# Decode attention over a long K/V cache: last chunk moved into the common loops, fewer score signals, VectorE loop head at slot 128, mask set by GpSimd

## The chip, the cores and the metric

The kernel runs on one core of a Trainium2 chip. The metric is device time in microseconds (us), median of several executions. Besides the time, each kernel left a profile of one execution: busy times, waits, and the start and end of every instruction and of every DMA packet. Engines are PE (TensorE matmuls), PEld (TensorE weight loads), DVE (VectorE), ACT (ScalarE), POOL (GpSimd) and SP (SyncE, which here only issues transfers). "SPq" and "DVEq" are the sequencers of those engines.

## The reference

One token, 16 query heads, 8 K/V heads, a cache of 65,536 positions by 256 values, all bf16. Attention is mixed by a scalar gate with a small MLP, which GpSimd and ScalarE do on the side and which plays no part in the argument.

```python
q = (x @ wq).reshape(B, Sq, Hq, Dh)                    # 16 heads of 256, D = 448
scores = einsum("bhqd,bhkd->bhqk", q, k) * Dh ** -0.5  # k, v: 8 heads, each for 2 query heads
p = softmax(scores)
a = einsum("bhqk,bhkd->bhqd", p, v).reshape(...) @ wo
out = g * a + (1 - g) * mlp(x)                         # g = sigmoid((x * gate_w).sum())
```

K and V together are 537 MB, read once. Next to that the arithmetic is small.

## The kernel before

The cache is cut into 48 chunks: 8 heads ("turns") of 6 chunks each, with 6, 6, 5, 5, 5 and 5 steps of 2048 positions. There are two K buffers and one V buffer. For each chunk VectorE transposes K step by step into three small buffers `kT`, TensorE computes 8 score matmuls per step, ScalarE takes the exponential, VectorE transposes the result, and TensorE multiplies it by V. VectorE's addition of that product (`drain_pv`) raises `s_vf`; this releases the V buffer, and SyncE then issues the next V and K loads together.

```python
def load_k(i):
    if i >= 2: sp.wait_ge(s_vf, i - 1)
    sp.dma_start(out=kbuf[i % 2][...], in_=kv_src(A_k_cache, i))
def load_v(i):
    if i >= 1: sp.wait_ge(s_vf, i + 1)
    sp.dma_start(out=vbuf[...], in_=kv_src(A_v_cache, i))

plan = [(0, 1), (1, 2), (2, 0), (3, 1), (5, 2), (4, 0)]   # (step, kT buffer)
def turns(i):                                             # VectorE
    take(dve, s_k[i % 2], 16)                             # K chunk landed
    for t, (s, b) in enumerate(blocks(i)):
        if t >= 3:                                        # a kT buffer is used again
            take(dve, s_s, 6 - steps[i] + 1 if t == steps[i] - 1 else 1)
        dve.transpose(out=kT[b], in_=step s of K).then_inc(s_kt, 1)
# scores(): steps 0, 1 and 2 each raise s_s when their last matmul is done

with nc.Fori(0, HKV, 1, engines=[DVE], head_slot={DVE: 0}) as turn_v:
    for c in range(PER):
        turns(c)
        ...                                               # drain_pv -> s_vf; transpose of p -> s_pt
# TensorE: loop over 47 chunks (scores 0..3, p_v of the chunk before, last scores);
# the 48th chunk is written out again after the loop, with its own probability buffer
```

`head_slot` is the loop's parameter for the slot at which its first instruction is placed. The rest of the kernel is unchanged, apart from its tail shown in the diff.

The softmax here doesn't subtract the row's maximum and nothing guards it: scores larger than these inputs give would overflow.

Of the kernel before, what the change touches and what calls it, by code (L numbers as in the profile page):

```python
# [9 lines left out]
BF16 = mybir.dt.bfloat16  # L10
# [5 lines left out]
HKV = 8  # L16
DH = 256
# [77 lines left out]
def kernel(  # L95
# [78 lines left out]
    pT_t = [const.tile([128, 512], BF16, name=f"pT{i}") for i in range(2)]  # L174
# [32 lines left out]
    def critical():  # L207
# [12 lines left out]
        s_d = nc.alloc_semaphore("s_d")  # L220
        s_g = nc.alloc_semaphore("s_g")
# [52 lines left out]
        )  # L274
        do("pool", lambda e: e.memset(block[:], 0.0), writes=["block"])
# [5 lines left out]
        do("pool", lambda e: e.memset(ymix[:], 0.0), writes=["ymix"])  # L281
        for t, key, val in (
            (one_b, "one_b", 1.0), (xd, "xd", 0.0), (one_f, "one_f", 1.0), (zero_b, "zero_b", 0.0),
            (xw, "xw", 0.0), (pat, "pat", 0.0), (qw, "qw", 0.0), (col_f, "col_f", 1.0), (pv, "pv", 0.0),
        ):
            do("dve", lambda e: e.memset(t[:], val), writes=[key])
# [141 lines left out]
        for m, spans in offsets.items():  # L428
            for lo, hi in spans:
                do("dve", lambda e: e.memset(pat[:, m, lo:hi], 1.0), writes=["pat"])  # L430
# [91 lines left out]
        def turns(i):  # L522
            kn = kbuf[i % 2][:].bitcast(FP32)
            take(dve, s_k[i % 2], 16)
            for t, (s, b) in enumerate(blocks(i)):
                if t >= 3:
                    take(dve, s_s, 6 - steps[i] + 1 if t == steps[i] - 1 else 1)
                dve.transpose(  # L528
                    out=kT[b][:].bitcast(FP32), in_=kn[:, s * SB * 128:(s + 1) * SB * 128]
                ).then_inc(s_kt, 1)  # L530
# [32 lines left out]
        with nc.Fori(0, HKV, 1, engines=[DVE], head_slot={DVE: 0}) as turn_v:  # L563
            for c in range(PER):
                turns(c)
                if c == 0:
                    with dve.If_ne(t_reg, 0):
                        take(dve, s_pv)
                        take(dve, s_d)
                        drain_pv(False).then_inc(s_vf, 1)  # L570
                        dve.memset(tick[:], 0.0).then_inc(s_g, 1)
                    with dve.Else():
                        dve.memset(og[:], 0.0).then_inc(s_vf, 1)
                    take(dve, s_e)
                    dve.transpose(out=pT_t[0][:], in_=p_t[:]).then_inc(s_pt, 1)  # L575
                    with dve.If_ne(t_reg, 0):
                        take(dve, s_o)
                        rden_gate(o_ps[:, 0, 2:4])
                        take(dve, s_wo, 16)
                        heads().then_inc(s_ot, 1)  # L580
                elif c < PER - 1:
                    take(dve, s_pv)
                    drain_pv(c == 1).then_inc(s_vf, 1)
                    take(dve, s_e)
                    dve.transpose(out=pT_t[0][:], in_=p_t[:]).then_inc(s_pt, 1)  # L585
                else:
                    with dve.If_lt(t_reg, HKV - 1):
                        take(dve, s_pv)
                        drain_pv(False).then_inc(s_vf, 1)
                        take(dve, s_e)  # L590
                        dve.transpose(out=pT_t[0][:], in_=p_t[:]).then_inc(s_pt, 1)  # L591
                        for r in range(2):
                            queries(turn_v + 1, r)
                        den_rows()
                        dve.tensor_scalar(
                            out=og[:], in0=og[:], scalar1=dsum[:, 0:1], scalar2=None, op0=ALU.add
                        ).then_inc(s_d, 1)
                    with dve.Else():
                        take(dve, s_e)
                        dve.transpose(out=pT_t[1][:], in_=p_t[:]).then_inc(s_pt, 1)  # L600
            dve.reg_add(t_reg, t_reg, 1)
# [54 lines left out]
        def scores(s, b, first, last):  # L656
            pe.wait_ge(s_kt, 1).then_inc(s_kt, -1)  # L657
            kv = kT[b][:].rearrange("p (j b y two) -> p j b y two", j=SB, b=4, two=2)
            at = PAD - ROW0 - s
            for q in range(8):  # L660
                ins = pe.matmul(  # L661
                    sc[:], lhsT=qw[:, q, at:at + 128], rhs=kv[:, :, q // 2, :, q % 2],
                    start=(first and q == 0), stop=(last and q == 7), skip_group_check=True,
                )
            if last:
                ins.then_inc(s_sc, 1)
            elif s < 3:
                ins.then_inc(s_s, 1)
# [29 lines left out]
        g_reg = pe.alloc_register("g_reg")  # L698
        f_reg = pe.alloc_register("f_reg")
        pe.reg_mov(c_reg, 0)  # L700
        pe.reg_mov(v_reg, PER)
        pe.reg_mov(g_reg, PER + 1)
        pe.reg_mov(f_reg, 1)
        with nc.Fori(0, total - 1, 1, engines=[PE], head_slot={PE: 0}):
            for s, b in plan[0:4]:
                scores(s, b, s == 0, False)
            with pe.If_lt(f_reg, 1):
                pe.wait_ge(s_pt, 1).then_inc(s_pt, -1)
                pe.wait_ge(s_v, 16).then_inc(s_v, -16)  # L709
                for s in range(4):  # L710
                    p_v(vbuf, pT_t[0], s, s == 0, False)
                with pe.If_lt(v_reg, big):
                    p_v(vbuf, pT_t[0], 5, False, False)
                p_v(vbuf, pT_t[0], 4, False, True).then_inc(s_pv, 1)
            pe.reg_mov(f_reg, 0)
# [3 lines left out]
            pe.reg_mov(v_reg, c_reg)  # L719
            pe.reg_add(c_reg, c_reg, 1)  # L720
            with pe.If_eq(c_reg, PER):
                pe.reg_mov(c_reg, 0)
            pe.reg_add(g_reg, g_reg, -1)
            with pe.If_lt(g_reg, 1):
                pe.reg_mov(g_reg, PER)
                pe.wait_ge(s_g, 1).then_inc(s_g, -1)
                o_turn(4).then_inc(s_o, 1)
                pe.wait_ge(s_ot, 1).then_inc(s_ot, -1)  # L728
                for k in range(4):
                    cc, r = divmod(k, 2)  # L730
                    ins = pe.matmul(  # L731
                        acc[0:1, 0:D], lhsT=oT[:, k:k + 1], rhs=wo[:, r, cc, :], start=False,
                        stop=False, skip_group_check=True,
                    )
                ins.then_inc(s_oo, 1)

# [3 lines left out]
        for t, (s, b) in enumerate(blocks(last_i)):  # L740
            scores(s, b, t == 0, t == steps[-1] - 1)
        take(pe, s_pt)
        take(pe, s_v, 16)
        for s in range(steps[-2]):
            p_v(vbuf, pT_t[0], s, s == 0, False)
        then(dve.tensor_tensor(out=dmul[:], in0=den[:], in1=dmask, op=ALU.mult))
        dve.tensor_reduce(out=dsum[:], in_=dmul[:], axis=AXIS.X, op=ALU.add).then_inc(s_fd, 1)
        pe.wait_ge(s_fd, 1)
        pe.matmul(
            den_ps[:, 0:2], lhsT=dsum[:].to_broadcast([128, 128]), rhs=mask[:, D0:D0 + 2, 0],  # L750
            start=True, stop=True,
        ).then_inc(s_fp, 1)
        pe.wait_ge(s_mp, 6 * NF)
        pe.matmul(
            acc[0:1, 0:D], lhsT=col_f[:], rhs=ymix[:], start=False, stop=True, skip_group_check=True,
        ).then_inc(s_fp, 1)
        dve.wait_ge(s_fp, 1)
        rden_gate(den_ps[:, 0:2])
        dve.wait_ge(s_fp, 2)
        dve.tensor_scalar(  # L760
            out=row[:], in0=acc[0:1, 0:D], scalar1=bias[:, 0:1], scalar2=None, op0=ALU.add
        ).then_inc(s_fd, 1)

        pTk = pT_t[1][:].rearrange("p (i b x) -> p i b x", b=4, x=16)
        pTr = pT_t[1][:].rearrange("p (j r x) -> p j r x", r=2, x=16)

        def upright(lo, hi):
            for jj in range(lo, hi, 2):
# [4 lines left out]
                    rhs=vlast[:, jj * DH:(jj + 2) * DH], start=False, stop=jj >= nlast - TURN - 8,  # L773
# [14 lines left out]

        take(pe, s_pt)
        pe.wait_ge(s_last[0], 16)  # L790
        upright(edges[0], edges[1])
        pe.wait_ge(s_fd, 2)
# [5 lines left out]
        pe.wait_ge(s_last[1], 16)  # L798
        upright(edges[1], edges[2]).then_inc(s_fp, 1)
        dve.wait_ge(s_fp, 3)  # L800
        drain_pv(False).then_inc(s_fd, 1)
        pe.wait_ge(s_fd, 3)
        o_turn(2)
        pe.wait_ge(s_last[2], 16)
        turned(edges[2], edges[3])
        pe.wait_ge(s_last[3], 16)
        turned(edges[3], edges[4]).then_inc(s_fp, 1)
        dve.wait_ge(s_fp, 4)
        heads().then_inc(s_fd, 1)
        pe.wait_ge(s_fd, 4)  # L810
# [11 lines left out]
        dve.wait_ge(s_fp, 5)  # L822
        dve.tensor_copy(out=res[0:97, :], in_=acc4[0:97, 0:DQ]).then_inc(s_fd, 1)  # L823
        s_out = nc.alloc_semaphore("s_out")
        sp.wait_ge(s_fd, 5)
# [37 lines left out]
```

## Time and profile before

| what | number |
|---|---|
| time, median of the first 3 runs | 1268.05 us (1266.36 to 1268.35) |
| span of the profiled run | 1264.1 us |
| HBM read | 544.22 MB, 431 GB/s over the span |

These lines are from the page of the kernel before: busy time and share of the span, the DMA row in 40 slices (9 is 90% or more), and the K/V queue.

```profile
PE 721.0 (57%) x4296; PEld 282.0 (22%) x4296; DVE 666.8 (53%) x471; ACT 50.1 (4%) x127; POOL 76.7 (6%) x98
DMA  9999999999999999999999999999999999999998
q1 hardware_dynamic: 16744, 544.22, 99.7%
```

No compute engine is busy much over half of the time. The queue that carries K and V is busy throughout. The table by window (columns: window, length, busy time of each engine with instruction counts, granted TensorE clock, DMA share, GB/s) says the same for the stretches between the two ends, again for the kernel before:

```profile
20.00:100.00 80.00, 46.03 (x244) 17.37 (x243) 48.29 (x29) 2.71 (x7) 1.69 (x2) 0.80 1.01 434
100.00:1220.00 1120.00, 639.52 (x3768) 249.36 (x3767) 590.84 (x381) 44.48 (x113) 72.17 (x81) 0.78 1.00 434
```

One steady chunk of the kernel before, in the timeline (start, length, engine, line, operation, count, and in brackets the idle time before it with what ended it):

```profile
1211.07 8.89 DVE L528 STREAM_TRANSPOSE kT<-kbuf 128x2048 f32<-128x2048 f32 x4 [6.34 <-DVEq L520]
1213.53 9.39 PE L661 MATMUL sc<-kT,qw 128*128 128x512 bf16 x32 [10.38 <-PEq L657]
1221.34 2.31 DVE L528 STREAM_TRANSPOSE kT<-kbuf 128x2048 f32<-128x2048 f32 x1 [1.37 <-DVEq L520]
1225.65 0.69 DVE L539 TENSOR_TENSOR og<-pv,og 128x512 f32<-128x512 f32 x1 [2.00 <-DVEq L520]
1226.37 0.33 SPq L247 DMA_DIRECT2D vbuf<-in_A_v_cache_dram  x1
```

VectorE waits 6.34 us for K to land, does four transpositions without a break, and 14.6 us after the first one the drain releases the next V load. In the same timeline the start of the program and the end look like this; the second line is the third K chunk's load, the third the second V chunk's:

```profile
31.50 13.28 DVE L528 STREAM_TRANSPOSE kT<-kbuf 128x2048 f32<-128x2048 f32 x6 [5.82 <-DVEq L520]
45.35 0.34 SPq L241 DMA_DIRECT2D kbuf<-in_A_k_cache_dram  x1
63.13 0.33 SPq L247 DMA_DIRECT2D vbuf<-in_A_v_cache_dram  x1
...
1258.84 1.43 PE L782 MATMUL misc<-pT,kbuf 128*128 128x2 bf16 x48 [0.56 <-DMA kbuf<-in_A_v_cache_dram]
1260.30 0.16 DVE L546 TENSOR_TENSOR oT<-misc,rden 128x4 bf16<-128x4 f32 x1 [3.18 <-PE misc L782]
1260.52 0.54 PE L816 MATMUL acc<-wo,oT 128*1 128x112 bf16 x16 [0.25 <-DVE oT L546]
1261.11 0.28 DVE L823 CAST res<-acc 97x112 bf16<-97x112 f32 x1 [0.65 <-PE acc L816]
```

After the last V rows land at about 1258.8 us, 5.3 us remain to the end of the span.

A number used below is the **cover** of an issue. It is the time from the issue of a V chunk to the landing of the last packet of the K chunk queued ahead of it, read from the trace's packet records. While the cover is well above zero, the queue has bytes left when the new load arrives. In the kernel before, the second V chunk, issued at 63.1 us, has a cover of 6.8 us. From the ninth V chunk on the least is about 6.3 and the median about 8.4 us (there from the landing signals, which in these traces come 0.3 to 0.5 us after the last packet).

### The profile page before, as it was taken

What the parts mean: (1) busy time and instruction counts of PE and PEld (TensorE: products, weight loads), DVE (VectorE), ACT (ScalarE), POOL (GpSimd) and SP (SyncE); (2) the same over time, 40 slices, a digit from 0 to 9 for tenths busy, and PEclk for the clock granted to TensorE, in tenths of its full rate; (3) what the DMA queues carried; (4) which work ended last, traced back from release to release, by engine and by line L of the source; (5) the groups of instructions that cost most, each with busy time, mean ns of one, the idle gap of its engine ahead of it and who ended that gap; (6) DMA issues with size and microseconds to landing.
All of it is one profiled execution on the core that took longest, in us unless ns stands there. A gap on an engine that the chain in (4) does not pass through costs nothing. (4 is left out here: it accounts for less than half of the span.)

```text
span 1264.1 us, 10739 instructions
## 1 busy us (share of the span) xinstructions
PE 721.0 (57%) x4296; PEld 282.0 (22%) x4296; DVE 666.8 (53%) x471; ACT 50.1 (4%) x127; POOL 76.7 (6%) x98
## 2 busy tenths in 40 slices
PE   3755655456555665556554564566645755456556
PEld 1321222122221222212221221222212222122212
DVE  4845555365544645455555554465545654466444
ACT  0000000000000000000000000000000000000000
POOL 0001010110101101001011011000000000000000
PEclk9876788778777787777887788777877787778887
DMA  9999999999999999999999999999999999999998
GB/s 407 424 439 430 437 438 425 438 434 428 440 437 423 434 436 433 440 430 435 434 429 435 430 435 440 430 429 437 430 440 435 430 431 435 427 443 435 424 435 350
DMA packets 16842, 544.32 MB, mean 431 GB/s; under 512 B 1856, under 2 KB 3906, under 8 KB 4162
## 3 DMA queue, kind: packets, MB, share of 16 engines
q1 hardware_dynamic: 16744, 544.22, 99.7%
q8 instruction: 3, 0.05, 0.0%
q14 instruction: 5, 0.04, 0.0%
q10 hardware_dynamic: 90, 0.01, 0.0%
HBM read 544.22 MB, written 0.00 MB: 431 GB/s over the span
## 5 line engine op out<-in xcount | busy, mean ns | idle before, releaser
L661 PE MATMUL sc<-kT,qw 128*128 128x512 bf16 x2048 | 564.5, 438 | 458.6 <-PEq L657 458.6
L528 DVE STREAM_TRANSPOSE kT<-kbuf 128x2048 f32<-128x2048 f32 x256 | 571.1, 2283 | 310.7 <-DVEq L520 310.7
L661 PEld LDWEIGHTS sc<-kT,qw 128*128 128x128 bf16 x2048 | 213.7, 108 | 807.7 <-issue 644.1
L675 PE MATMUL pv<-vbuf,pT 128*4 128x512 bf16 x2008 | 130.5, 412 | 54.6 <-PEq L709 54.2
L539 DVE TENSOR_TENSOR og<-pv,og 128x512 f32<-128x512 f32 x39 | 27.0, 692 | 108.8 <-DVEq L520 106.3
L675 PEld LDWEIGHTS pv<-vbuf,pT 128*4 128x4 bf16 x2008 | 50.6, 92 | 132.4 <-issue 92.9
L608 ACT ACTIVATE p_t<-sc 128x512 bf16<-128x512 f32 x48 | 28.7, 597 | 1190.0 <-PE sc L661 1190.0
L585 DVE STREAM_TRANSPOSE pT<-p_t 128x512 bf16<-128x512 bf16 x32 | 22.8, 711 | 74.3 <-DVEq L520 74.3
L635 POOL TENSOR_SCALAR t_b<-t_b 128x448 f32<-128x448 f32 x14 | 7.9, 566 | 359.9 <-ACT t_b L617 359.9
L639 POOL TENSOR_SCALAR t_b<-t_b,hw 128x448 f32<-128x448 f32 x14 | 9.0, 640 | 333.4 <-ACT t_b L625 333.4
L538 DVE COPY og<-pv 128x512 f32<-128x512 f32 x8 | 5.5, 692 | 35.4 <-DVEq L520 35.4
L575 DVE STREAM_TRANSPOSE pT<-p_t 128x512 bf16<-128x512 bf16 x8 | 5.7, 711 | 26.9 <-DVEq L520 26.9
L644 POOL TENSOR_TENSOR ymix<-ymix,t_b 128x448 f32<-128x448 f32 x14 | 16.1, 1149 | 1.1
L643 POOL TENSOR_TENSOR t_b<-t_b,u_b 128x448 f32<-128x448 f32 x14 | 15.8, 1128 | 1.2
L638 POOL TENSOR_TENSOR t_b<-t_b,u_b 128x448 f32<-128x448 f32 x14 | 15.8, 1127 | 1.2
L731 PE MATMUL acc<-wo,oT 128*1 128x448 bf16 x28 | 7.0, 374 | 12.7 <-PEq L728 12.7
L591 DVE STREAM_TRANSPOSE pT<-p_t 128x512 bf16<-128x512 bf16 x7 | 5.0, 711 | 13.1 <-DVEq L520 13.1
L617 ACT ACTIVATE t_b<-h_bc,b1T,w1T 128x448 f32<-128x448 f32 x14 | 10.5, 747 | 0.0
L631 POOL TENSOR_SCALAR u_b<-h_bc,w1T,b1T 128x448 f32<-128x448 f32 x14 | 10.0, 718 | 4.1 <-DVE pat L430 2.7
L608 ACT ACTIVATION_READ_ACCUMULATOR p_t<-sc 128x1 f32 x48 | 9.3, 194 | 0.0
L685 PEld LDWEIGHTS misc<-mask,og 128*128 128x128 f32 x64 | 8.7, 196 | 2.3 <-DVE og L539 1.3
L448 PE MATMUL sc<-vbuf,xw 128*128 128x512 bf16 x32 | 9.0, 449 | 0.0
(89 smaller groups left out, 70.3 us busy)
## 6 DMA issues: line engine op xcount, KB each, us to landing
kbuf<-in_A_k_cache_dram SPq DMA_DIRECT2D x32, 5120.0 KB, 33.2
vbuf<-in_A_v_cache_dram SPq DMA_DIRECT2D x31, 5120.0 KB, 20.8
kbuf<-in_A_k_cache_dram SPq DMA_DIRECT2D x16, 6144.0 KB, 36.1
vbuf<-in_A_v_cache_dram SPq DMA_DIRECT2D x16, 6144.0 KB, 24.2
wo<-in_A_wo_dram SPq DMA_DIRECT2D x7, 448.0 KB, 22.3
vbuf<-in_A_wq_dram SPq DMA_DIRECT2D x1, 3072.0 KB, 10.2
kbuf<-in_A_v_cache_dram SPq DMA_DIRECT2D x1, 2560.0 KB, 26.5
kbuf<-in_A_v_cache_dram SPq DMA_DIRECT2D x1, 1280.0 KB, 31.1
```

The costliest lines, as they stand in the source:

```text
L448: last = e.matmul(q_ps[:], lhsT=xw[:, k, HKV - 1 - n:HKV - 1 - n + 128], rhs=rhs, start=(n == 0 and k == 0), stop=(n == HKV - 1 and k >= K ...
L528: dve.transpose(out=kT[b][:].bitcast(FP32), in_=kn[:, s * SB * 128:(s + 1) * SB * 128]).then_inc(s_kt, 1)
L539: return dve.tensor_tensor(out=og[:], in0=pv[:], in1=og[:], op=ALU.add)
L585: dve.transpose(out=pT_t[0][:], in_=p_t[:]).then_inc(s_pt, 1)
L608: ins = act.activation(out=p_t[:], in_=sc[:], func=ACT.Exp, scale=scale, accum_out=den[:, c:c + 1])
L617: ins = act.activation(out=t_b[:], in_=h_bc[:], func=ACT.Square, scale=w1T[:, b:b + 1], bias=b1T[:, b:b + 1],)
L631: lambda: pool.tensor_scalar(out=u_b[:], in0=h_bc[:], scalar1=w1T[:, b:b + 1], scalar2=b1T[:, b:b + 1], op0=ALU.mult, op1=ALU.add,),
L638: lambda: pool.tensor_tensor(out=t_b[:], in0=t_b[:], in1=u_b[:], op=ALU.mult),
L643: lambda: pool.tensor_tensor(out=t_b[:], in0=t_b[:], in1=u_b[:], op=ALU.mult),
L644: lambda: pool.tensor_tensor(out=ymix[:], in0=ymix[:], in1=t_b[:], op=ALU.add),
L661: ins = pe.matmul(sc[:], lhsT=qw[:, q, at:at + 128], rhs=kv[:, :, q // 2, :, q % 2], start=(first and q == 0), stop=(last and q == 7), ski ...
L675: ins = pe.matmul(pv[32 * a:32 * a + 4, :], lhsT=pT[:, k, :, ROW0 + s], rhs=vt[:, j * DH:(j + 2) * DH], start=first and k < 4, stop=last a ...
```

## The change

The intent is to run all 48 chunks through one TensorE loop and one VectorE loop body, with fewer signals and less VectorE work in the preamble. The diff, cut to its core:

```diff
-with nc.Fori(0, HKV, 1, engines=[DVE], head_slot={DVE: 0}) as turn_v:
+with nc.Fori(0, HKV, 1, engines=[DVE], head_slot={DVE: 128}) as turn_v:
 ...
-                if t >= 3:
-                    take(dve, s_s, 6 - steps[i] + 1 if t == steps[i] - 1 else 1)
+                if t in (3, steps[i] - 1):
+                    take(dve, s_s)
 ...  in scores():
-            elif s < 3:
+            elif s in (1, 2):
                 ins.then_inc(s_s, 1)
 ...  VectorE, sixth chunk of a turn: the special case of the last turn is gone;
 ...  denominator rows now come ahead of the next head's queries
 ...  TensorE
-        with nc.Fori(0, total - 1, 1, engines=[PE], head_slot={PE: 0}):
+        with nc.Fori(0, total, 1, engines=[PE], head_slot={PE: 0}):
-        for t, (s, b) in enumerate(blocks(last_i)):
-            scores(s, b, t == 0, t == steps[-1] - 1)
-        ...  p_v of chunk 46
 ...  tail: drain of chunk 46 is in the loop, so upright() starts a new sum (start=jj < 8);
 ...  the four matmuls on `row` move from between the two upright() calls to after turned()
 ...  preamble: the 11 memsets of `pat`, and those of zero_b and col_f, on GpSimd, not VectorE
```

With three signals, transposition 3 (the fourth) waited for score step 0. With two, it waits for score step 1, since one signal is now counted for both.

More of the change, by code (lines that the diff above doesn't have):

```diff
@@ L173 @@
     p_t = const.tile([128, 512], BF16, name="p_t")
-    pT_t = [const.tile([128, 512], BF16, name=f"pT{i}") for i in range(2)]
+    pT = const.tile([128, 512], BF16, name="pT")
     den = const.tile([128, PER], FP32, name="den")
@@ L220, in critical @@
         s_d = nc.alloc_semaphore("s_d")
+        s_dn = nc.alloc_semaphore("s_dn")
         s_g = nc.alloc_semaphore("s_g")
@@ L274, in critical @@
         )
+        do("pool", lambda e: e.memset(pat[:], 0.0), writes=["pat"])
+        for m, spans in offsets.items():
+            for lo, hi in spans:
+                do("pool", lambda e: e.memset(pat[:, m, lo:hi], 1.0), writes=["pat"])
         do("pool", lambda e: e.memset(block[:], 0.0), writes=["block"])
@@ L281, in critical @@
         do("pool", lambda e: e.memset(ymix[:], 0.0), writes=["ymix"])
+        do("pool", lambda e: e.memset(zero_b[:], 0.0), writes=["zero_b"])
+        do("pool", lambda e: e.memset(col_f[:], 1.0), writes=["col_f"])
         for t, key, val in (
-            (one_b, "one_b", 1.0), (xd, "xd", 0.0), (one_f, "one_f", 1.0), (zero_b, "zero_b", 0.0),
-            (xw, "xw", 0.0), (pat, "pat", 0.0), (qw, "qw", 0.0), (col_f, "col_f", 1.0), (pv, "pv", 0.0),
+            (one_b, "one_b", 1.0), (xd, "xd", 0.0), (xw, "xw", 0.0), (one_f, "one_f", 1.0),
+            (qw, "qw", 0.0), (pv, "pv", 0.0),
         ):
@@ L425, in critical @@
         )
-        for m, spans in offsets.items():
-            for lo, hi in spans:
-                do("dve", lambda e: e.memset(pat[:, m, lo:hi], 1.0), writes=["pat"])
         do(
@@ L568, in critical @@
                         take(dve, s_pv)
-                        take(dve, s_d)
+                        take(dve, s_dn)
                         drain_pv(False).then_inc(s_vf, 1)
@@ L574, in critical @@
                     take(dve, s_e)
-                    dve.transpose(out=pT_t[0][:], in_=p_t[:]).then_inc(s_pt, 1)
+                    dve.transpose(out=pT[:], in_=p_t[:]).then_inc(s_pt, 1)
                     with dve.If_ne(t_reg, 0):
@@ L584, in critical @@
                     take(dve, s_e)
-                    dve.transpose(out=pT_t[0][:], in_=p_t[:]).then_inc(s_pt, 1)
+                    dve.transpose(out=pT[:], in_=p_t[:]).then_inc(s_pt, 1)
                 else:
-                    with dve.If_lt(t_reg, HKV - 1):
-                        take(dve, s_pv)
-                        drain_pv(False).then_inc(s_vf, 1)
-                        take(dve, s_e)
-                        dve.transpose(out=pT_t[0][:], in_=p_t[:]).then_inc(s_pt, 1)
-                        for r in range(2):
-                            queries(turn_v + 1, r)
-                        den_rows()
-                        dve.tensor_scalar(
-                            out=og[:], in0=og[:], scalar1=dsum[:, 0:1], scalar2=None, op0=ALU.add
-                        ).then_inc(s_d, 1)
-                    with dve.Else():
-                        take(dve, s_e)
-                        dve.transpose(out=pT_t[1][:], in_=p_t[:]).then_inc(s_pt, 1)
+                    take(dve, s_pv)
+                    drain_pv(False).then_inc(s_vf, 1)
+                    take(dve, s_e)
+                    dve.transpose(out=pT[:], in_=p_t[:]).then_inc(s_pt, 1)
+                    den_rows()
+                    dve.tensor_scalar(
+                        out=og[:], in0=og[:], scalar1=dsum[:, 0:1], scalar2=None, op0=ALU.add
+                    ).then_inc(s_dn, 1)
+                    for r in range(2):
+                        queries(turn_v + 1, r)
             dve.reg_add(t_reg, t_reg, 1)
@@ L697, in critical @@
         v_reg = pe.alloc_register("v_reg")
-        g_reg = pe.alloc_register("g_reg")
-        f_reg = pe.alloc_register("f_reg")
         pe.reg_mov(c_reg, 0)
         pe.reg_mov(v_reg, PER)
-        pe.reg_mov(g_reg, PER + 1)
-        pe.reg_mov(f_reg, 1)
-        with nc.Fori(0, total - 1, 1, engines=[PE], head_slot={PE: 0}):
+        with nc.Fori(0, total, 1, engines=[PE], head_slot={PE: 0}):
             for s, b in plan[0:4]:
                 scores(s, b, s == 0, False)
-            with pe.If_lt(f_reg, 1):
+            with pe.If_lt(v_reg, PER):
                 pe.wait_ge(s_pt, 1).then_inc(s_pt, -1)
@@ L710, in critical @@
                 for s in range(4):
-                    p_v(vbuf, pT_t[0], s, s == 0, False)
+                    p_v(vbuf, pT, s, s == 0, False)
                 with pe.If_lt(v_reg, big):
-                    p_v(vbuf, pT_t[0], 5, False, False)
-                p_v(vbuf, pT_t[0], 4, False, True).then_inc(s_pv, 1)
-            pe.reg_mov(f_reg, 0)
+                    p_v(vbuf, pT, 5, False, False)
+                p_v(vbuf, pT, 4, False, True).then_inc(s_pv, 1)
             with pe.If_lt(c_reg, big):
@@ L718, in critical @@
             scores(4, 0, False, True)
-            pe.reg_mov(v_reg, c_reg)
-            pe.reg_add(c_reg, c_reg, 1)
-            with pe.If_eq(c_reg, PER):
-                pe.reg_mov(c_reg, 0)
-            pe.reg_add(g_reg, g_reg, -1)
-            with pe.If_lt(g_reg, 1):
-                pe.reg_mov(g_reg, PER)
+            with pe.If_eq(v_reg, PER - 1):
                 pe.wait_ge(s_g, 1).then_inc(s_g, -1)
@@ L735, in critical @@
                 ins.then_inc(s_oo, 1)
+            pe.reg_mov(v_reg, c_reg)
+            pe.reg_add(c_reg, c_reg, 1)
+            with pe.If_eq(c_reg, PER):
+                pe.reg_mov(c_reg, 0)
         s_fd = nc.alloc_semaphore("s_fd")
         s_fp = nc.alloc_semaphore("s_fp")
-        for t, (s, b) in enumerate(blocks(last_i)):
-            scores(s, b, t == 0, t == steps[-1] - 1)
-        take(pe, s_pt)
-        take(pe, s_v, 16)
-        for s in range(steps[-2]):
-            p_v(vbuf, pT_t[0], s, s == 0, False)
-        then(dve.tensor_tensor(out=dmul[:], in0=den[:], in1=dmask, op=ALU.mult))
-        dve.tensor_reduce(out=dsum[:], in_=dmul[:], axis=AXIS.X, op=ALU.add).then_inc(s_fd, 1)
-        pe.wait_ge(s_fd, 1)
-        pe.matmul(
-            den_ps[:, 0:2], lhsT=dsum[:].to_broadcast([128, 128]), rhs=mask[:, D0:D0 + 2, 0],
-            start=True, stop=True,
-        ).then_inc(s_fp, 1)
-        pe.wait_ge(s_mp, 6 * NF)
-        pe.matmul(
-            acc[0:1, 0:D], lhsT=col_f[:], rhs=ymix[:], start=False, stop=True, skip_group_check=True,
-        ).then_inc(s_fp, 1)
-        dve.wait_ge(s_fp, 1)
-        rden_gate(den_ps[:, 0:2])
-        dve.wait_ge(s_fp, 2)
-        dve.tensor_scalar(
-            out=row[:], in0=acc[0:1, 0:D], scalar1=bias[:, 0:1], scalar2=None, op0=ALU.add
-        ).then_inc(s_fd, 1)
-        pTk = pT_t[1][:].rearrange("p (i b x) -> p i b x", b=4, x=16)
-        pTr = pT_t[1][:].rearrange("p (j r x) -> p j r x", r=2, x=16)
+        pTk = pT[:].rearrange("p (i b x) -> p i b x", b=4, x=16)
+        pTr = pT[:].rearrange("p (j r x) -> p j r x", r=2, x=16)
         def upright(lo, hi):
@@ L772, in upright @@
                     pv[32 * a:32 * a + 4, :], lhsT=pTk[:, j // 2, :, ROW0 + s],
-                    rhs=vlast[:, jj * DH:(jj + 2) * DH], start=False, stop=jj >= nlast - TURN - 8,
+                    rhs=vlast[:, jj * DH:(jj + 2) * DH], start=jj < 8, stop=jj >= nlast - TURN - 8,
                     tile_position=(0, 32 * a), skip_group_check=True,
@@ L787, in turned @@
             return ins
+        pe.wait_ge(s_mp, 6 * NF)
+        pe.matmul(
+            acc[0:1, 0:D], lhsT=col_f[:], rhs=ymix[:], start=False, stop=True, skip_group_check=True,
+        )
         take(pe, s_pt)
@@ L791, in critical @@
         upright(edges[0], edges[1])
+        take(pe, s_dn)
+        pe.matmul(
+            den_ps[:, 0:2], lhsT=dsum[:].to_broadcast([128, 128]), rhs=mask[:, D0:D0 + 2, 0],
+            start=True, stop=True,
+        ).then_inc(s_fp, 1)
+        dve.wait_ge(s_fp, 1)
+        rden_gate(den_ps[:, 0:2])
+        pe.wait_ge(s_last[1], 16)
+        upright(edges[1], edges[2]).then_inc(s_fp, 1)
+        dve.wait_ge(s_fp, 2)
+        drain_pv(False).then_inc(s_fd, 1)
+        dve.tensor_scalar(
+            out=row[:], in0=acc[0:1, 0:D], scalar1=bias[:, 0:1], scalar2=None, op0=ALU.add
+        ).then_inc(s_fd, 1)
+        pe.wait_ge(s_fd, 1)
+        o_turn(2)
+        pe.wait_ge(s_last[2], 16)
+        turned(edges[2], edges[3])
+        pe.wait_ge(s_last[3], 16)
+        turned(edges[3], edges[4]).then_inc(s_fp, 1)
+        dve.wait_ge(s_fp, 3)
+        heads().then_inc(s_fd, 1)
         pe.wait_ge(s_fd, 2)
@@ L797, in critical @@
             )
-        pe.wait_ge(s_last[1], 16)
-        upright(edges[1], edges[2]).then_inc(s_fp, 1)
-        dve.wait_ge(s_fp, 3)
-        drain_pv(False).then_inc(s_fd, 1)
         pe.wait_ge(s_fd, 3)
-        o_turn(2)
-        pe.wait_ge(s_last[2], 16)
-        turned(edges[2], edges[3])
-        pe.wait_ge(s_last[3], 16)
-        turned(edges[3], edges[4]).then_inc(s_fp, 1)
-        dve.wait_ge(s_fp, 4)
-        heads().then_inc(s_fd, 1)
-        pe.wait_ge(s_fd, 4)
         for k in range(4):
@@ L821, in critical @@
         ins.then_inc(s_fp, 1)
-        dve.wait_ge(s_fp, 5)
+        dve.wait_ge(s_fp, 4)
         dve.tensor_copy(out=res[0:97, :], in_=acc4[0:97, 0:DQ]).then_inc(s_fd, 1)
         s_out = nc.alloc_semaphore("s_out")
-        sp.wait_ge(s_fd, 5)
+        sp.wait_ge(s_fd, 4)
         sp.dma_start(
```

## The prediction

> **What bounds the kernel now.** The transfers. The profile's DMA queue section gives the K/V queue 99.7% of 16 engines' span for 544.22 MB, 431 GB/s. The table by window shows DMA share 1.00 and 434 GB/s in both long stretches (60 to 660 us, 660 to 1226 us), while PE is busy 57% and DVE 53% (busy section). The queue shows no idle gap. Only the ends can change the time: about 1 us before the first transfer, and in the timeline 1258.8 us (last V rows landed) to 1264.1 us: turned product 1.44 us, heads 0.17, projection 0.57, copy 0.28, output DMA and close about 2.7.
>
> **Slack in the steady loop.** In the late timeline the drain of chunk 45 (0.69 us) frees V and the next pair is issued at 1202.18 us, while the K chunk already queued lands only at 1211.07: 8.9 us of queued bytes cover the issue. DVE then sits idle about 6.3 us for K in each chunk (waits by engine: transposes wait 310.7 us in all, longest 7.5).
>
> **What the change does.**
> 1. Fewer score signals: transposition 3 now waits for score step 1 instead of step 0. A transposition is 2.28 us, 8 score matmuls about 2.35 us (32 in 9.39). Step 1 ends about 2.4+4.7=7.1 us after K landed, where DVE is ready at 6.9; cost 0.2 to 0.4 us per chunk, inside 6 to 8 us of slack.
> 2. Queries after the denominator rows: swapped before a K wait of 6 us. Zero.
> 3. VectorE loop head at slot 128: [...] In the before trace the first transposition starts at 31.5 us although K0's packets ended at about 26.6[...]. Either way zero.
> 4. Preamble: ten mask memsets (1.24 us) leave DVE. The projection that frees V's buffer ends at 21.9 us, but K0 and K1 keep the queue busy until about 42 us. Zero.
> 5. Tail: p_v of chunk 46 (2.33 us), its drain (0.69) and the denominator add (0.75) now come in the loop, before and after the last score step. I expect chunk 47's transposition of the probabilities about 2 us later (1250.6 to about 1252.5) and its first upright product at about the same 1253.3; V's last parts land at 1255.8 and 1258.8, so this is nearly hidden. The four row matmuls (0.37 us) now stand behind the turned product, partly under heads: +0.1 to +0.3 us. [...]
>
> **Predicted time:** 1268.3 us against 1268.05; 8 in 10 between 1265.5 and 1271.5. Chances: faster by over 2%: 0.01, within 2%: 0.97, slower by over 2%: 0.02.
>
> **What would show each step right.** DMA share 1.00 and 434 GB/s in the same windows; last V rows landing within 1 us of before; DVE's first transposition near 27 us with the K2 issue earlier, yet the later landings unmoved; the last K chunk's timeline with p_v between the fourth and fifth score steps.
>
> **What would make it wrong.** A fetch stall at each turn beyond about 6 us, which would show as a gap on the K/V queue; a different DMA rate from moved buffers; a DVE fetch stall over 2 us in the tail.

Steps 1 to 4 counted zero and step 5 0.1 to 0.3 us, which with 1268.05 gives 1268.3. The cut parts of step 3 put the start some 5 us earlier (my estimate from 31.5 and 26.6 us in the trace of the kernel before), or else an instruction packet in each of the 8 turns (my estimate from the 16 KB ones in that trace, 0.97 us each). "Either way" means these two; both were counted as zero.

## The result, and the profile after

The changed kernel takes 1265.97 us (1265.64 to 1266.17, 4 runs) against 1267.2 us (1266.27 to 1268.35, 4 runs) for the kernel before, so the times are the same. The ratio is 0.999 with a 95% interval of 0.9972 to 1.0007. Ratios in this document are the mean time of one kernel's fast runs over that of the other's fast runs of the same rounds, so they are not quite the ratio of the medians quoted.

The same lines from the page after, and the same two windows:

```profile
PE 722.2 (57%) x4296; PEld 276.3 (22%) x4296; DVE 675.3 (53%) x462; ACT 50.1 (4%) x127; POOL 78.5 (6%) x111
DMA  9999999999999999999999999999999999999998
q1 hardware_dynamic: 16744, 544.22, 99.7%
...
20.00:100.00 80.00, 46.18 (x243) 17.18 (x242) 48.74 (x29) 2.71 (x7) 1.69 (x2) 0.82 1.01 434
100.00:1220.00 1120.00, 640.91 (x3768) 244.22 (x3767) 597.17 (x381) 44.45 (x113) 72.04 (x81) 0.79 1.00 434
```

The queue is as busy as before, and the windows show the same 434 GB/s. The steady chunk in the timeline after is not the same:

```profile
1210.87 6.70 DVE L532 STREAM_TRANSPOSE kT<-kbuf 128x2048 f32<-128x2048 f32 x3 [5.63 <-DVEq L524]
1213.33 7.50 PE L661 MATMUL sc<-kT,qw 128*128 128x512 bf16 x24 [9.67 <-PEq L657]
1219.24 4.50 DVE L532 STREAM_TRANSPOSE kT<-kbuf 128x2048 f32<-128x2048 f32 x2 [1.67 <-DVEq L524]
1226.03 0.69 DVE L543 TENSOR_TENSOR og<-pv,og 128x512 f32<-128x512 f32 x1 [2.29 <-DVEq L524]
1226.75 0.33 SPq L248 DMA_DIRECT2D vbuf<-in_A_v_cache_dram  x1
```

VectorE now stops after three transpositions for 1.67 us, and the drain comes 15.2 us after the first one, where it was 14.6. Start and end in the timeline after:

```profile
27.17 6.70 DVE L532 STREAM_TRANSPOSE kT<-kbuf 128x2048 f32<-128x2048 f32 x3 [1.65 <-DVEq L524]
42.46 0.34 SPq L242 DMA_DIRECT2D kbuf<-in_A_k_cache_dram  x1
62.46 0.33 SPq L248 DMA_DIRECT2D vbuf<-in_A_v_cache_dram  x1
...
1258.62 1.44 PE L751 MATMUL misc<-pT,kbuf 128*128 128x2 bf16 x48 [0.54 <-DMA kbuf<-in_A_v_cache_dram]
1259.99 0.55 PE L789 MATMUL acc<-row,one_f 1*1 1x112 f32 x8
1260.09 0.16 DVE L550 TENSOR_TENSOR oT<-misc,rden 128x4 bf16<-128x4 f32 x1 [2.60 <-PE misc L751]
1260.46 0.54 PE L799 MATMUL acc<-wo,oT 128*1 128x112 bf16 x16
1261.06 0.27 DVE L806 CAST res<-acc 97x112 bf16<-97x112 f32 x1 [0.81 <-PE acc L799]
```

The first transposition starts 4.3 us earlier and the third K chunk is issued 2.9 us earlier, yet the second V chunk only 0.7 us earlier (cover 7.3 us in place of 6.8). At the end the row matmuls stand in the way: from the start of the turned product to the end of the span (1264.1) it takes 5.5 us in place of 5.3.

### The profile page after: what moved, and what is told of

It reads as the page before. It is cut to its first block, busy times and chain, and to the rows that moved or that the text cites. A ratio compares the mean times of both kernels' runs of the same rounds, so it can differ in the third digit from the quotient of the medians.

```text
span 1264.1 us, 10623 instructions
## 1 busy us (share of the span) xinstructions
PE 722.2 (57%) x4296; PEld 276.3 (22%) x4296; DVE 675.3 (53%) x462; ACT 50.1 (4%) x127; POOL 78.5 (6%) x111
## 3 DMA queue, kind: packets, MB, share of 16 engines
q1 hardware_dynamic: 16744, 544.22, 99.7%
HBM read 544.22 MB, written 0.00 MB: 431 GB/s over the span
## 5 line engine op out<-in xcount | busy, mean ns | idle before, releaser
L661 PE MATMUL sc<-kT,qw 128*128 128x512 bf16 x2048 | 573.5, 438 | 482.9 <-PEq L657 482.9
L661 PEld LDWEIGHTS sc<-kT,qw 128*128 128x128 bf16 x2048 | 211.1, 108 | 845.1 <-issue 692.8
L675 PE MATMUL pv<-vbuf,pT 128*4 128x512 bf16 x2008 | 121.2, 390 | 28.8 <-PEq L705 28.7
L675 PEld LDWEIGHTS pv<-vbuf,pT 128*4 128x4 bf16 x2008 | 47.1, 88 | 99.3 <-issue 53.8
L720 PE MATMUL acc<-wo,oT 128*1 128x448 bf16 x28 | 10.1, 504 | 12.7 <-PEq L717 12.7
L477 DVE TENSOR_TENSOR qw<-qr,block 128x32 bf16<-128x32 f32 (+1 forms) x18 | 8.6, 561 | 0.1
(86 smaller groups left out, 77.4 us busy)
## 6 DMA issues: line engine op xcount, KB each, us to landing
kbuf<-in_A_k_cache_dram SPq DMA_DIRECT2D x32, 5120.0 KB, 33.2
```

The source lines that it names most:

```text
L661: ins = pe.matmul(sc[:], lhsT=qw[:, q, at:at + 128], rhs=kv[:, :, q // 2, :, q % 2], start=(first and q == 0), stop=(last and q == 7), ski ...
L675: ins = pe.matmul(pv[32 * a:32 * a + 4, :], lhsT=pT[:, k, :, ROW0 + s], rhs=vt[:, j * DH:(j + 2) * DH], start=first and k < 4, stop=last a ...
L720: ins = pe.matmul(acc[0:1, 0:D], lhsT=oT[:, k:k + 1], rhs=wo[:, r, cc, :], start=False, stop=False, skip_group_check=True,)
```

## The experiments

The theory: the transfers bound the kernel from the first packet to the last, and everything that the change moves on VectorE and TensorE stays inside the cover. The rivals: VectorE or TensorE time does count, and the parts of the change cancel; or the slot costs or saves time by itself. Twelve kernels ran. All passed the comparison with the reference, even the two that leave work out; the comparison is thus not sensitive to what those two leave out. The kernel before, on the chips of these three batches, had medians of 1266.41, 1266.48 and 1266.35 us. The changed kernel itself was not run again there; its 1265.97 us is from the first comparison.

### Fewer bytes, and less TensorE work

`a_vless` is the changed kernel with the last step's 4096 values per partition left out of the V loads of the second to the 47th chunk (a wrong result; the last chunk is loaded in parts elsewhere and stays whole):

```diff
+            if i:
+                n -= SB * DH
-            sp.dma_start(out=vbuf[:, 0:n], in_=kv_src(A_v_cache, i)).then_inc(s_v, 16)
+            sp.dma_start(out=vbuf[:, 0:n], in_=kv_src(A_v_cache, i)[:, 0:n]).then_inc(s_v, 16)
```

> The changed kernel loading 16 columns of heads less per V chunk from the second on (wrong result on purpose: old values stay in the buffer): 49.3 MB of 544.2 fewer. Theory (the transfers bound it at 434 GB/s): 49.3/0.434 = 114 us less, 1148 to 1160 us. Rival (VectorE or TensorE bounds it): 1266 us, or clearly less than 114 us saved.

Measured: 1156.4 us (1156.15 to 1156.74), ratio 0.9131. HBM read falls to 495.99 MB. The time falls by 110 us where the missing bytes alone give 111 us (544.22 - 495.99 = 48.2 MB over 434 GB/s). The expectation had 49.3 MB because it counted the last chunk too.

`a_halfpe` is the changed kernel with every second score matmul left out (a wrong result):

```diff
-            for q in range(8):
+            for q in range(0, 8, 2):
 ...  stop= moves from q == 7 to q == 6
```

> The changed kernel with every second score matmul left out (wrong result on purpose), about 285 of 722 us of TensorE work. Theory: 1265 to 1267 us, DMA share 1.00 as before. Rival (TensorE's pace sets the issue times that count): faster by over 0.5%.

Measured: 1265.58 us, ratio 0.9996 (0.998 to 1.0011). From the pages of the two kernels, first the one with fewer bytes, then the one with fewer matmuls:

```profile
HBM read 495.99 MB, written 0.00 MB: 430 GB/s over the span
```

```profile
PE 582.6 (46%) x3272; PEld 175.8 (14%) x3272; DVE 672.9 (53%) x462; ACT 50.1 (4%) x127; POOL 78.7 (6%) x111
HBM read 544.22 MB, written 0.00 MB: 431 GB/s over the span
```

Removing 9% of the bytes removes 9% of the time. Removing 140 us of TensorE busy time removes none. The bound by transfers is thereby shown, not only read from the busy row. (My expectation took 285 us of busy time off; half the matmuls took only half of that off. Those left took 509 ns each on average in place of 438, at a granted clock of 0.70 in that run in place of 0.80.)

### How much VectorE work fits: doses

A reduction over a broadcast zero is put ahead of every chunk. It writes a value that nobody reads.

```diff
+                dve.tensor_reduce(
+                    out=zout[:], in_=zin[:].to_broadcast([128, N]), axis=AXIS.X, op=ALU.add
+                )
                 turns(c)
```

N = 3700, 5450 and 7100 measured 3.97, 5.79 and 7.51 us each.

> The changed kernel with one extra VectorE reduction of about 4.0 us ahead of each of the 48 chunks, 192 us of added VectorE work. Theory (the transfers bound it; VectorE sits idle 32.5 us in a turn of six chunks just before its chunks' first transpositions, and 6 x 4.0 = 24 us fits in): within 0.5% of the changed kernel's 1266 us. Rival (the change stayed level because VectorE time was saved and spent again, so VectorE work counts): up to +190 us.

> The same with a reduction of about 5.75 us: 34.5 us a turn against 32.5 us of idle in the changed kernel. Theory (the merged score signals used up about 2.3 us of VectorE slack a turn): exposed by about 2 us a turn, +5 to +20 us over 1266, and slower than the kernel before with the same dose. Rival (no slack was used): the same time as the kernel before with the same dose.

> The kernel before with the same 5.75 us reduction: 34.5 us a turn against 34.8 us of idle measured in it. Theory: at the edge, 0 to +8 us over 1267, less than the changed kernel with this dose. Rival: equal to it.

> The changed kernel with a reduction of about 7.5 us: 45 us a turn against 32.5 us. Theory: VectorE now bounds the loop, about (45-32.5) x 8 = +100 us, less some 6 us of queue slack, so 1340 to 1375 us, and gaps on the K/V queue with a rate well under 434 GB/s. Rival (the transfer rate is set elsewhere and VectorE never matters): 1266 us.

Measured:

| kernel | dose per chunk | time, us | second V chunk issued, us | its cover, us | gap on the queue near 70 us |
|---|---|---|---|---|---|
| changed | 0 | 1266.0 | 62.5 | 7.3 | none |
| a_dose4 | 3.97 us | 1269.74 | 69.2 | 0.7 | 0.27 us |
| a_dose5 | 5.79 us | 1273.97 | 73.1 | -3.2 | 4.2 us |
| b_dose5 (kernel before) | 5.79 us | 1277.26 | 75.3 | -5.4 | 6.3 us |
| a_dose7 | 7.51 us | 1332.83 | 77.4 | -7.5 | 8.5 us, and smaller ones later |

The 190 us of work added by the smallest dose cost 3.8 us, of which 3 us is the 420 GB/s in place of 433 between 20 and 120 us, the gap included. That much of the theory holds, and the rival falls. Two expectations missed in kind. First, I looked for the loss of the 5.79 us dose in the steady loop. The traces of both kernels with this dose have only one gap, near 70 us, and from 120 us on both run at 433 to 434 GB/s. The loss is the start: the second V chunk is issued late, and after it the cover recovers. In all four rows with a gap, the gap is 0.9 to 1.0 us longer than the negative cover, which is the time from that issue to its first packet. Second, the kernel before lost more than the changed one, the reverse of what I expected. The next runs say why. Two times also lay outside their ranges: `b_dose5` is 10 us over 1267 where 0 to 8 was expected, and `a_dose7` is 7 us under its 1340. For `a_dose5`, the table by window shows the loss at the start and the full rate after it:

```profile
20.00:120.00 100.00, 54.17 (x279) 20.38 (x276) 79.11 (x37) 2.71 (x7) 1.69 (x2) 0.78 0.95 402
120.00:660.00 540.00, 301.71 (x1826) 115.47 (x1828) 410.25 (x208) 26.03 (x63) 56.95 (x64) 0.79 1.00 433
660.00:1220.00 560.00, 311.71 (x1900) 120.37 (x1888) 416.15 (x211) 18.49 (x50) 15.27 (x17) 0.79 1.00 433
```

Only the largest dose makes VectorE the bound: in turns 2 to 8 its first transposition of a chunk follows the dose without a pause, 4.5 us or more after the K chunk has landed. The table by window of `a_dose7` has a lower rate in the whole middle:

```profile
120.00:660.00 540.00, 288.83 (x1727) 109.84 (x1725) 419.20 (x192) 24.88 (x60) 53.27 (x60) 0.76 0.98 412
660.00:1220.00 560.00, 307.62 (x1848) 117.93 (x1848) 437.33 (x212) 18.26 (x49) 18.94 (x21) 0.77 0.99 418
```

### The slot of the VectorE loop head

All are the changed kernel but for what is named; `a_slot0_dose5` adds the 5.79 us dose, `a_slot0_oldsig` the old score signals.

```diff
-        with nc.Fori(0, HKV, 1, engines=[DVE], head_slot={DVE: 128}) as turn_v:
+        with nc.Fori(0, HKV, 1, engines=[DVE], head_slot={DVE: 0}) as turn_v:     # 192 in a_slot192
```

> The changed kernel with the VectorE loop head back at slot 0 of its block. Theory (the slot is what moved the first transposition from 31.5 to 27.2 us, and the queue covers it): first transposition back near 31.5 us, the issue of the third K chunk back near 45 us from 42.5, time unchanged within 0.2% of 1266 us. Rival (the shorter preamble moved it): first transposition stays near 27 us.

> The changed kernel with the VectorE loop head at slot 192[...]. Theory: either no stall, or a fetch each turn that shows as at least 8 more instruction packets and a later transposition once a turn, but under the 6 to 8 us by which each issue is ahead of the queue's end, so time within 0.3% of 1266 us. Rival[...]: slower by more than 0.5%.

> The changed kernel with the 5.79 us reduction per chunk and the head at slot 0. Theory (the kernel before lost more under this dose because its loop starts some 4 us later, and the start is where the queue first runs dry): slower than the changed kernel with this dose by 1.5 to 4.5 us, with a larger single gap on the K/V queue near 70 us. Rival (some other part of the change made the difference): the same as the changed kernel with this dose, 1274 us.

> The changed kernel with slot 0 and the old score signals. Theory (slot 0 alone cost 2 to 3 us in the changed kernel because the late start and the merged signals together leave only 1.4 us of queued bytes when the second V chunk is issued near 68 us): with the old signals that issue falls near 63 to 66 us with 4 us or more of cover, first transposition still at 31 to 33.5 us, time 1265.5 to 1267. Rival (slot 0 costs its 2 to 3 us by itself): 1268.3 us again.

Measured:

| kernel | slot | signals | first transposition, us | second V chunk issued, us | cover, us | time, us |
|---|---|---|---|---|---|---|
| before | 0 | old | 31.5 | 63.1 | 6.8 | 1266.4 (median on these chips) |
| changed | 128 | new | 27.2 | 62.5 | 7.3 | 1266.0 |
| a_slot192 | 192 | new | 27.2 | 61.3 | 8.5 | 1266.17 |
| a_slot0 | 0 | new | 33.4 | 68.5 | 1.4 | 1268.32 |
| a_slot0_oldsig | 0 | old | 31.8 | 64.9 | 5.2 | 1266.26 |
| a_dose5 | 128 | new | dosed | 73.1 | -3.2 | 1273.97 |
| a_slot0_dose5 | 0 | new | dosed | 76.8 | -6.9 | 1280.35 |

From the timeline and the table by window of `a_slot0`:

```profile
33.35 6.70 DVE L532 STREAM_TRANSPOSE kT<-kbuf 128x2048 f32<-128x2048 f32 x3 [7.14 <-DVEq L524]
68.47 0.33 SPq L248 DMA_DIRECT2D vbuf<-in_A_v_cache_dram  x1
...
20.00:100.00 80.00, 45.34 (x244) 17.05 (x242) 47.13 (x28) 2.71 (x7) 1.69 (x2) 0.83 0.99 423
100.00:1220.00 1120.00, 638.70 (x3763) 243.51 (x3764) 597.90 (x381) 44.46 (x113) 72.04 (x81) 0.79 1.00 433
```

The slot decides when the loop starts, and the shorter preamble does not: at slot 0 every undosed kernel waits until 31.5 to 33.4 us, after 5.8 to 7.1 us of idle VectorE time, at 128 and 192 until 27.2, after 1.4 to 1.7 us. At slot 0 with the new signals, only 1.4 us of cover is left. The queue is not empty at any moment, but between 20 and 100 us it moves 423 GB/s in place of 434, which is about 2 us (11/434 of 80 us). So a cover of 1.4 us is already too little, because it counts the last packet alone: 14 of the 16 DMA engines had finished that K chunk by 68.8 us, the last packet landed at 69.9, and the first packets of the new V chunk started at 69.4 and took 2.0 to 3.6 us each, where in the changed kernel they take 1.8. All four runs of `a_slot0` (1267.6 to 1269.0) lie above all four of `a_slot192` on the same chip (1265.8 to 1266.3); against the kernel before, which on that chip has one run at 1268.18: ratio 1.0012 (0.9996 to 1.0029). With the old signals slot 0 costs nothing that the runs can show. So within the changed kernel the slot is worth about 2 us (192 against 0 on one chip; the changed kernel's own time at 128 agrees), and it pays for a late start that shows in the time only together with the new signals. It also explains the kernel before's larger loss under the dose: its loop starts later. The two slot 0 kernels with the 5.79 us dose lost 3.3 and 6.4 us more than the one at slot 128. The 6.4 us is above the 1.5 to 4.5 expected; the gap near 70 us accounts for 3.6 of it (7.8 us in place of 4.2), and the rest is not explained. In `a_slot0` the third K chunk was issued at 49.65 us, also later than the 45 expected.

What the late start waits for was not shown; the traces give these times. VectorE's last preamble instruction ends at 25.5 to 26.2 us in these kernels. K's first chunk has its last packet at 26.6 us in the kernel before. In the slot 0 kernels there is an instruction packet of 8 KB about 2 us ahead of the first transposition (29.5 us in the kernel before, 31.3 in `a_slot0`) and another at 35.8 to 37.5 us. The latter is missing in the slot 128 and 192 kernels, which do not wait for the former. That the start waits for the former packet is my guess from these times; no run tests it. The time of that packet also varied by 1.8 us between slot 0 runs (29.5 and 31.3 us), so the difference between `a_slot0` and `a_slot0_oldsig` is not all due to the signals: of the 3.5 us between their issues of the second V chunk, 1.6 us is the later first transposition, and 2.0 us comes after it (35.1 us from there to the issue in place of 33.2). There is one trace per kernel, so it isn't known how the other runs started.

`a_slot192` was made to see whether a still later head brings an instruction packet each turn. It costs nothing that the runs can show, and after 40 us it has one instruction packet more than the changed kernel, not eight.

### What the merged signals cost

`a_oldsig_dose7` is `a_dose7` with the old signals. VectorE bounds `a_dose7`, so anything that holds VectorE up shows in the time.

```diff
-                if t in (3, steps[i] - 1):
-                    take(dve, s_s)
+                if t >= 3:
+                    take(dve, s_s, 6 - steps[i] + 1 if t == steps[i] - 1 else 1)
-            elif s in (1, 2):
+            elif s < 3:
```

> The changed kernel with the 7.51 us reduction per chunk, where VectorE bounds the loop, but with the old score signals (three a chunk, the fourth transposition waits for the first score step). Theory (the merged signals cost VectorE 0.2 to 0.4 us a chunk, which is hidden without a dose): faster than the changed kernel with this dose by 10 to 20 us, 1313 to 1323 us. Rival (they cost nothing even where VectorE bounds): 1333 us.

Measured: 1275.37 us against 1332.83 us for `a_dose7`, each against the same kernel before (ratios 1.0067 and 1.0524). The direction is the one expected, the size is far larger: 57 us, or 1.2 us a chunk. It is also a lower limit, since `a_oldsig_dose7` is back at the transfers' pace (its main gap on the queue is the one at the start, 4.6 us, and then its rate is 433 GB/s where `a_dose7` has 412 and 418):

```profile
120.00:660.00 540.00, 291.83 (x1805) 114.13 (x1804) 443.62 (x207) 26.03 (x63) 56.94 (x64) 0.76 1.00 433
660.00:1220.00 560.00, 311.63 (x1918) 122.45 (x1916) 450.59 (x211) 18.49 (x50) 15.27 (x17) 0.77 1.00 433
```

The trace of the undosed kernels says why I was off. These are means over turns 2 to 8 of the fifth chunk, in us from its first transposition:

| | transposition 3 starts | score step 1 ends | transposition 4 starts | last score step ends |
|---|---|---|---|---|
| before | 6.62 | 8.35 | 10.25 | 16.34 |
| changed | 8.35 | 8.20 | 10.59 | 16.84 |

In the chunk shown above (first transposition near 1211 us) the first 10 or 11 matmuls start 0.43 us apart and the rest 0.22 us apart, in both traces; in other chunks 6 to 15 are slow. I had taken the mean of 32, so I had score step 1 end at 7.1 us; it ends at 8.2 (7.6 to 8.8 in the seven turns of the changed kernel). Both traces show the slow spacing at the head of all 48 chunks, after 3.9 to 12.8 us of idle TensorE time (9.67 and 10.38 us before the chunk shown). After the pause of about 0.87 us that each chunk of the changed kernel has later on, the score matmuls start 0.22 us apart at once, in all 48. Why the first ones are slow was not tested. So transposition 3 waits for a matmul group that comes after, or among, matmuls at the slow spacing.

### The tail, and a version with both undone

`a_oldsig_row` is the changed kernel with the old signals and with the row matmuls back ahead of the turned product:

```diff
         o_turn(2)
+        pe.wait_ge(s_fd, 2)
+        ...  the four matmuls acc4 <- row
         pe.wait_ge(s_last[2], 16)
         turned(edges[2], edges[3])
         ...
-        pe.wait_ge(s_fd, 2)
-        ...  the four matmuls acc4 <- row
```

> The changed kernel with the old score signals and the four row matmuls moved back ahead of the turned product. Theory (the transfers bound it): within 0.1% of 1266 us; from the start of the turned product to the end of the span 5.3 us instead of 5.5; the fourth transposition of a chunk starts 6.6 us after the first again instead of 8.35. Rival (the merged signals cost time in the undosed kernel): faster by more than 2 us.

Measured: 1265.7 us (1265.46 to 1266.83), ratio 0.9996 (0.9982 to 1.0009). Its turned product starts at 1258.60 us and the span ends at 1263.9, which is 5.3 us. Transposition 3 starts at 6.62 us again, and the second V chunk has a cover of 9.0 us, the best of all kernels here. None of it shows in the time beyond 0.3 us, which is within the scatter. There is no version here that clearly beats both kernels.

## Why the prediction was right

- **Bound, and time.** Predicted 1268.3 us (1265.5 to 1271.5), measured 1265.97 us. The transfers bound the kernel, as `a_vless` and `a_halfpe` show. The forecast of no change was right because in both kernels every K and V load is issued with bytes still queued. The middle is 2.3 us too high; I had taken over the median of the first three runs of the kernel before, two of which lay near 1268, while its later medians were 1266.4.
- **Step 1, the signals.** The mechanism and the conclusion (hidden) were right. The term "step 1 ends about 2.4+4.7=7.1 us after K landed" was mis-sized: it ends at 8.2 us, because the first matmuls of a chunk start 0.43 us apart and not 0.22. The "cost 0.2 to 0.4 us per chunk" measured 0.5 us at the chunk's last score step undosed and at least 1.2 us where VectorE is the bound.
- **Step 2, the order of queries and denominator rows.** No run isolates it, nor the merged loop. Nothing in the traces speaks against zero.
- **Step 3, the slot.** The start near 27 us was right (27.2), and `a_slot0` shows that the slot causes it. "Either way zero" was wrong as a statement on that part alone: in the changed kernel slot 128 is worth about 2 us. It is zero against the kernel before because that kernel, with the old signals, had 6.8 us of cover in the same place. An instruction packet each turn did not come at any slot that was tried: after 40 us the trace of the changed kernel has four of them in eight turns, `a_slot192` one more, and the kernel before, at slot 0, five.
- **Step 4, the preamble.** The projection's end and the V load behind it moved by 0.2 us (21.90 to 21.74), and nothing followed from that.
- **Step 5, the tail.** The transposition of chunk 47's probabilities came at 1252.6 us (predicted 1252.5) and its first upright product at 1253.5 (predicted 1253.3). The row matmuls cost 0.2 us (predicted 0.1 to 0.3). After the loop VectorE waits at most 0.81 us at a time, but for the 2.60 us until the turned product is done.
- **What I had not seen.** I gave one figure of slack for the steady loop and took the start for safe ("K0 and K1 keep the queue busy until about 42 us"). The dose runs show that the first place to run dry is the issue of the second V chunk near 63 us, and that the steady loop is more robust than the idle time before a chunk suggests: 5.79 us more per chunk left it at full rate. With that dose the cover of the second V chunk fell from 7.3 us to -3.2, while the least from the ninth V chunk on went only from about 7.1 us to about 6.6.

## What to carry to other kernels

When one queue is busy from end to end, cost a change by how early each load is issued ahead of the queue's end, and look for the margin that shrinks fastest when work is added. Here it was the one at the start of the program, though without a dose it was no smaller than the least in the steady loop (6.8 us against 6.3 in the kernel before). A change that moves no time can still spend or add margin, and two parts can cancel; add a dose of work that brings the engine to its limit, and the parts become measurable. Take the time of a matmul group from the place in the chunk where it stands, not from the mean, when TensorE has been idle before it: here the first 6 to 15 matmuls after 3.9 to 12.8 us of idle time started 0.43 us apart, the rest 0.22.
